# New order of the first two stages of a fused attention and feed-forward kernel: first chunk's squares ahead of all else on ScalarE, fewer dummy matmuls ahead of the first transposes

## Chip, cores, metric

One NeuronCore of a Trainium2 chip. The metric is the device time in microseconds (us) of one execution. Every run quoted here is of the fast state; a profile is of one such run. A ratio is the mean time of one kernel's fast runs over the mean of the other's in the same rounds, so it is not quite the ratio of the medians quoted beside it.

## What is computed

```python
# q, k, v: (8 batches, 12 heads, 448 rows, 64) float32
q_n, k_n = rmsnorm(q, g_q), rmsnorm(k, g_k)
attn = softmax(q_n @ k_n.T / 8) @ v                 # per batch and head
x = attn.transpose(0, 2, 1, 3).reshape(3584, 768)
h = x @ w_in                                        # 768 -> 2048
g = h + sin(alpha * h)**2 / (alpha + 1e-9)
out = g @ w_out                                     # 2048 -> 768
```

## The kernel before

It works batch by batch. Four heads of one batch are a *chunk*; batch b has chunks 3b, 3b+1, 3b+2 (counting from 0). The program order is not computed: it is written down as a *plan*, a string of tokens for batch 0 (STAGE_0), batch 1 (STAGE_1) and the rest (STAGE_N), a string of PSUM slots, and a table of tasks beside the first product. The first digit of most tokens is the chunk within the batch, 3 to 5 being the next batch's.

| token | engine | what |
|---|---|---|
| `L`, `G` | PE, then VectorE or ScalarE | spread alpha, spread g over the partitions |
| `l3` | SP | issue the loads of a chunk's q and k |
| `q30`, `q31` | ScalarE (chunks 0, 1), else GpSimd | squares of q, of k |
| `u30`, `u31` | VectorE | their row sums |
| `r3` | ScalarE | inverse root |
| `g3` | GpSimd | fold the gains g_q g_k into q, in place |
| `k30`, `k31` | VectorE (chunks 0 to 3), else GpSimd | scaled q, k in bf16 |
| `p3`, `t3` | PE with copies, or DMA | transpose |
| `S`, `S4` | PE, ScalarE | a score tile and its exponential; 4 dummy matmuls first |
| `b11` | PE | 11 dummy matmuls |
| `o v x y z` | PE | steps of (ones or values) x exponentials |
| `F` (a number: so many), `f` | PE | a filler: 8 matmuls of the batch before's second product |
| `W`, `O`, `V` | GpSimd | issue loads of w_in, w_out, v |
| `D2` | GpSimd | *gate*: copy one column of a chunk's k |

The gate does no arithmetic that anyone uses. GpSimd stops at it until that chunk's k has landed, so the weight loads that follow in GpSimd's order are issued later. In the changed kernel's profile only `D1` waits so: when `D2` and `D4` run (27.05 and 63.47 us), the k that they read has long landed (11.60 and 27.55). The parts that matter below (cuts marked ...):

```python
inp = ctx.enter_context(tc.tile_pool(name="inp", bufs=3))      # q and k of three chunks
...
    def load_qk(ci, k_queue=nc.sync):
        ...
        qk[ci] = inp.tile([P, 2, 2 * NJ, D], F32, tag="qk", name="qk")
...
        def square(w):
            if ci < 2:
                ...
                nc.scalar.activation(st.sq[w], qk[ci][:, w], ACT.Square)
            else:
                st.sq[w] = npool.tile([P, 2 * NJ, D], F32, tag="sq", name="sq")
                nc.gpsimd.tensor_mul(st.sq[w], qk[ci][:, w], qk[ci][:, w])
...
    def snake(b, ps, m):
        ...
        nc.scalar.activation(s1, hps, ACT.Sin, scale=alpha_sb[:, m, :])
        if m % 2 == 0:
            nc.gpsimd.tensor_mul(s2, s1, s1)
        else:
            nc.scalar.activation(s2, s1, ACT.Square)
        def finish():
            nc.vector.scalar_tensor_tensor(g_sb[...], s2, inv_alpha_sb[:, m, :], hps, ...)
            if m % 2:
                give_back(ps)          # PE may use the PSUM slot again
...
            if what == "D":
                nc.gpsimd.tensor_copy(gate, qk[ci][:, 1, 0, 0:1])
```

Three chunk buffers in turn: chunk 5's loads go where chunk 2 lies, chunk 7's where chunk 4 lies. A load waits until the last reader of the old chunk is done, and a gate is a reader.

The softmax here doesn't subtract the row's maximum and nothing guards it: scores larger than these inputs give would overflow.

Of the kernel before, what the change touches and what calls it, by code (L numbers as in the profile page):

```python
# [17 lines left out]
try:  # L18
# [12 lines left out]

STAGE_0 = (
    (
        "L G b11 q00 u00 q01 g0 b15 r00 u01 k00 r01 D1 k01 V00 q11 u11 p00 q10 V02 W11 p011 S4 u10 q20 r1 "
        "g1 S4 q21 S1 l3 u20 S1 k11 k10 S4 u21 S g2 r2 p1 k20 S2 V01 S2 S o3 q30 S W00 W12 k21 l4 o4 D2 "
        "q40 W01 p2 l5 S1 g4 S u30 q31 W02 g3 u40 v1 q41 S v6 u31 S S S3 S1 S3 x2 W10 S S x1 S1 u41 x2 y2 "
        "q51 y3 x2 z1 z1 y2 z1 z1 q50 r4 r3 z2 z1 O00 k31 "
    ),
    "2122130230213212301301321032130132012120312031230",
    {-1: 'u50 k30 u51 O01', 1: 'k401 O10', 2: 'k410 k411', 3: 'O11', 4: 'V10', 5: 'k400', 6: 'D4 l6 V11', 7: 'p3', 8: 'V12 g5 l7 p4'},  # L40
)
STAGE_1 = (
    (
        "q30 6 r2 1 S 4 S 1 S 2 S 2 u30 S k21 1 q41 1 S 1 f S 1 k20 1 S 1 S 1 f 1 S 1 f f f S q31 p2 1 "
        "u31 f l5 S 2 g3 S 2 S r3 2 u41 k30 V10 S 1 q40 1 V11 q50 S o7 v7 1 S k31 1 u40 S 2 S 3 S S 1 x6 "
        "r4 k41 z2 q51 x1 t3 y7 z5 "
    ),
    "13230103120101013131312310202302301230123",
    {-1: 'g4 V12', 1: 'k40', 3: 'u50 g5', 5: 'l6 u51', 8: 't4 l7'},
)  # L50
STAGE_N = (
    (
        "1 r2 q31 q30 f 2 S V10 f 3 V11 f f k20 2 S 3 S 2 k21 S u31 q40 1 t2 1 g3 1 S 1 f u30 S 2 f S f S "
        "r3 q41 f f 1 l5 1 f S 4 u40 S S 5 S S u41 o7 v7 S S 5 S 2 q51 f S 2 S q50 k31 k30 2 S g4 1 u50 S "
        "2 r4 t3 1 S z3 x7 k40 y7 z1 z2 z1 "
    ),
    "01232302102020301301320321310130210231023",
    {-1: 'l6 u51 V12', 1: 'k41', 2: 't4 l7', 3: 'g5'},
)
LAST = "0123012"  # L60

# [546 lines left out]
```

## Time and profile before

417.23 us median of 4 runs (416.84 to 417.42); the profiled span is 414.8 us.

| engine | busy share | what it does most |
|---|---|---|
| PE (TensorE) | 97% | products, scores, attention |
| ACT (ScalarE) | 76% | exponentials, sines |
| POOL (GpSimd) | 69% | squares, scalings, issues of loads |
| DVE (VectorE) | 55% | sums, copies out of PSUM |

The prediction shows the stretches, the chain and the run-in. Read so: over the whole span PE is the bound, but not in the first 39 us.

### The profile page before, as it was taken

Reading aid. Unit: us, or ns where it says so; the run is one execution under the profiler, and the core shown is the slowest. Engines: PE = TensorE matmul, PEld = TensorE weight load, DVE = VectorE, ACT = ScalarE, POOL = GpSimd, SP = SyncE. Lnnn points to the kernel's source line nnn. Section 1 sums busy time; section 2 is a strip of 40 time slices with the busy share of each in tenths; the row PEclk is TensorE's granted clock in tenths of the full one; section 3 lists DMA queues with packets and bytes.
Section 4 is the critical chain, followed back from the end, with each engine's and each line's share of the span. In section 5 each row is a group of like instructions: output and inputs, shape, how many; then the busy total and the mean of one; then the engine's idle time right before and its main releaser. Section 6 shows DMA issues by size and latency. Waiting matters only on the chain.

```text
span 414.8 us, 14996 instructions
## 1 busy us (share of the span) xinstructions
PE 403.4 (97%) x6657; PEld 238.9 (58%) x6657; DVE 227.2 (55%) x335; ACT 316.8 (76%) x465; POOL 285.0 (69%) x269
## 2 busy tenths in 40 slices
PE   4999999999999999999999999999999999999995
PEld 2344567655666557655666557655676556665563
DVE  2783774737754565655674565564565464435512
ACT  3698788968888689868889679878889688887600
POOL 3998998898869679498786879697794884003300
PEclk9999999999999999999999999999999999999999
DMA  8999999776273645567294744645375611320022
GB/s 257 176 220 241 168 226 217 167 155 174 29 206 93 150 134 103 158 90 193 70 182 112 175 136 88 172 111 149 92 135 162 89 45 44 82 60 2 1 77 76
DMA packets 64901, 54.07 MB, mean 130 GB/s; under 512 B 36276, under 2 KB 60612, under 8 KB 64836
## 3 DMA queue, kind: packets, MB, share of 16 engines
q1 hardware_dynamic: 51378, 39.60, 36.2%
q0 software_dynamic: 12512, 11.81, 19.3%
q10 hardware_dynamic: 946, 1.70, 1.1%
q8 instruction: 52, 0.85, 0.9%
q14 instruction: 13, 0.11, 0.1%
HBM read 45.62 MB, written 11.01 MB: 137 GB/s over the span
## 4 chain that ended last, share of the span: by engine, by line
PE 94%; ACT 3%; DMA 1%; issue 0%; DVE 0%; POOLq 0%
PE hps L401 35%; PE ops L480 30%; PE av L361 13%; PE sc L335 7%; PE ops L461 5%; ACT expT L338 3%; PE ps L243 2%; DMA small<-in_moe_alpha_dram 1%; PE sc L331 1%; PE tp L313 1%; ACT rec L367 0%; ACT rec L366 0%; PE aps L216 0%; DVE osb L466 0%; PE gps L209 0%
## 5 line engine op out<-in xcount | busy, mean ns | idle before, releaser
L338 ACT ACTIVATE expT<-sc 128x896 bf16<-128x896 f32 x168 | 144.6, 918 | 15.7 <-PE sc L335 15.1
L401 PE MATMUL hps<-xT,w_in 128*128 128x448 bf16 x768 | 146.7, 353 | 0.0
L480 PE MATMUL ops<-w_out_sb,g_sb 64*64 64x384 bf16 x3072 | 146.5, 323 | 0.0
L401 PEld LDWEIGHTS <-w_in 128*128 128x128 bf16 x768 | 74.4, 98 | 71.7 <-issue 3.0
L387 DVE SCALAR_TENSOR_TENSOR g_sb<-s,inv_alpha_sb,hps 128x448 bf16<-128x448 f32 x128 | 81.1, 677 | 62.8 <-POOL s L382 62.4
L480 PEld LDWEIGHTS <-g_sb 64*64 64x64 bf16 x3072 | 89.8, 107 | 39.4 <-issue 2.5
L382 POOL TENSOR_TENSOR s<-s 128x448 f32<-128x448 f32 x64 | 59.4, 932 | 66.9 <-ACT s L379 43.9
L379 ACT ACTIVATE s<-hps,alpha_sb 128x448 f32<-128x448 f32 x128 | 74.5, 626 | 38.4 <-PE hps L401 34.7
L265 POOL TENSOR_TENSOR sq<-qk 128x896 f32<-128x896 f32 x44 | 73.4, 1677 | 29.0 <-DMA qk<-in_k_dram 27.9
L290 POOL TENSOR_TENSOR qkn<-qk,inv 128x448 bf16<-128x448 f32 x80 | 72.8, 938 | 4.2 <-ACT inv L281 2.0
L335 PE MATMUL sc<-qkT 64*64 64x448 bf16 x672 | 57.1, 352 | 0.4 <-DVE qkT L320 0.2
L486 DVE COPY osb<-ops 128x384 f32<-128x384 f32 x48 | 26.7, 557 | 50.3 <-PE ops L480 50.3
L268 POOL TENSOR_TENSOR qk<-qk,gg 128x896 f32<-128x896 f32 x24 | 50.2, 2091 | 2.2 <-ACT g_sb L262 2.2
L271 DVE TENSOR_REDUCE ms<-sq 128x14 f32<-128x896 f32 x44 | 47.0, 1078 | 8.0 <-POOL sq L265 8.0
L373 DVE TENSOR_TENSOR xT<-av,rec 128x896 bf16<-128x896 f32 x24 | 25.4, 1088 | 33.7 <-ACT rec L367 33.7
L384 ACT ACTIVATE s<-s 128x448 f32<-128x448 f32 x64 | 36.9, 577 | 3.0
L361 PE MATMUL av<-expT,vb 64*32 64x448 bf16 (+1 forms) x1120 | 36.8, 350 | 0.1
L335 PEld LDWEIGHTS <-qkT 64*64 64x64 bf16 x672 | 20.2, 107 | 13.4 <-issue 4.5
L487 DVE TENSOR_TENSOR osb<-osb,ops 128x384 f32<-128x384 f32 x48 | 26.6, 554 | 1.7
L361 PEld LDWEIGHTS <-vb 64*32 64x32 bf16 (+1 forms) x1120 | 19.2, 96 | 13.2 <-issue 2.7
L361 PE MATMUL av<-expT,ones 64*32 64x448 bf16 (+1 forms) x672 | 25.3, 350 | 0.2 <-ACT expT L338 0.2
L461 PE MATMUL ops<-w_out_sb,g_sb 128*128 128x384 bf16 x128 | 21.0, 326 | 0.0
(48 smaller groups left out, 185.6 us busy)
## 6 DMA issues: line engine op xcount, KB each, us to landing
out_dram<-osb SPq DMA_DIRECT2D x39, 192.0 KB, 3.1
qk<-in_q_dram SPq DMA_DIRECT2D x16, 448.0 KB, 4.6
qk<-in_k_dram SPq DMA_DIRECT2D x14, 448.0 KB, 4.9
qk<-in_q_dram SPq DMA_DIRECT2D x16, 224.0 KB, 4.1
qk<-in_k_dram SPq DMA_DIRECT2D x16, 224.0 KB, 5.0
vb<-in_v_dram POOLq DMA_DIRECT2D x16, 224.0 KB, 4.4
w_out_sb<-in_moe_w_out_dram POOLq DMA_DIRECT2D x4, 768.0 KB, 12.8
out_dram<-osb SPq DMA_DIRECT2D x26, 96.0 KB, 3.6
```

The lines of the kernel that those rows point to most:

```text
L265: nc.gpsimd.tensor_mul(st.sq[w], qk[ci][:, w], qk[ci][:, w])
L268: eng.tensor_mul(qk[ci][:, 0], qk[ci][:, 0], gg.to_broadcast([P, 2 * NJ, D]))
L271: nc.vector.reduce_sum(st.ms[:, w, :], st.sq[w], axis=AX.X)
L290: eng.tensor_mul(n[:, :, hi, :], x[:, hi], inv[:, hi].unsqueeze(2).to_broadcast([P, NJ, D]))
L335: nc.tensor.matmul(sc[pp * 64:pp * 64 + 64, hi, :S], qkt[r, 1, j * REST:(j + 1) * REST], qkt[r, 0, :], start=True, stop=True)
L338: nc.scalar.activation(expT[c, j], sc[:, :, :S], ACT.Exp, scale=SCALE)
L361: nc.tensor.matmul(av[o, k, :S], w, expT[b * NC + c, j][r, hi, :], start=(j == 0), stop=(j == NJ - 1))
L379: nc.scalar.activation(s1, hps, ACT.Sin, scale=alpha_sb[:, m, :])
L382: nc.gpsimd.tensor_mul(s2, s1, s1)
L387: nc.vector.scalar_tensor_tensor(g_sb[:, m, (b % 2) * S:(b % 2 + 1) * S], s2, inv_alpha_sb[:, m, :], hps, op0=ALU.mult, op1=ALU.add)
L401: nc.tensor.matmul(ps[:, m % 2, :S], w_in_sb[m * 2 // MT][:, kt, m % (MT // 2) * P:(m % (MT // 2) + 1) * P], x[:, kt, :], start=(kt == ORD ...
L480: nc.tensor.matmul(st["ps"][os, r, :HALF], g_sb[rs, m, c0 + o * 64:c0 + o * 64 + 64], w_out_sb[rs, m, half * HALF:(half + 1) * HALF], star ...
```

## The change

The intent, as the diff reads: start batch 0 sooner. The first chunk's squares come first on ScalarE (`q01 q00` ahead of `G`, which holds the copy of g), the 15 dummies of `b15` go, two weight loads come first on GpSimd (`W02`, `W12`). Batch 1 does all its transposes by DMA. The plans of the later batches are new too, and so are the slots.

```diff
 STAGE_0 = (
     (
-        "L G b11 q00 u00 q01 g0 b15 r00 u01 k00 r01 D1 k01 V00 q11 u11 p00 q10 V02 W11 p011 S4 u10 q20 r1 "
-        "g1 S4 q21 S1 l3 u20 S1 k11 k10 S4 u21 S g2 r2 p1 k20 S2 V01 S2 S o3 q30 S W00 W12 k21 l4 o4 D2 "
-        "q40 W01 p2 l5 S1 g4 S u30 q31 W02 g3 u40 v1 q41 S v6 u31 S S S3 S1 S3 x2 W10 S S x1 S1 u41 x2 y2 "
-        "q51 y3 x2 z1 z1 y2 z1 z1 q50 r4 r3 z2 z1 O00 k31 "
+        "L q01 q00 G D1 u01 r01 u00 q11 W02 k01 b11 g0 q10 W12 r00 p011 q21 u11 k00 u10 g1 p00 q20 u21 r1 "
+        "k11 S4 S V00 g2 k10 V01 S2 u20 S1 l3 S3 q30 r2 p1 l4 S V02 S2 k20 k21 S1 S1 S3 S2 W00 S o7 W01 "
+        "p2 W11 b2 S D2 S S u30 v7 q41 W10 S S O01 u41 S1 q40 u40 l5 S1 q31 x3 S S1 z3 V10 O00 z2 x4 g3 "
+        "u31 y7 z2 r4 q51 r3 "
     ),
     ...
-    {-1: 'u50 k30 u51 O01', 1: 'k401 O10', 2: 'k410 k411', 3: 'O11', 4: 'V10', 5: 'k400', 6: 'D4 l6 V11', 7: 'p3', 8: 'V12 g5 l7 p4'},
+    {-1: 'k31 k30 g4', 0: 'q50 l6', 1: 'k401', 2: 'u50', 3: 'O10 k410', 5: 'k411 u51 k400', 7: 'g5 D4', 8: 'O11 p3 p4 V12 V11 l7'},
 )
 STAGE_1 = (
     (
-        "... S 1 f 1 S 1 f f f S q31 p2 1 u31 f l5 S 2 g3 ... "
+        "... f 1 S k21 f 1 S f t2 1 S 3 f S 1 u31 ... g3 f 1 S 1 V10 r3 l5 S g4 ... x2 u50 x4 x1 y1 l6 q51 ... "
     ),
     ...                                                  # slots, STAGE_N: new orders of the same work
```

## Prediction

> **What bounds the kernel now.** I read the page's table of busy shares first (PE 97%, ScalarE 76%, GpSimd 69%), then stretches cut at the borders of the stages, then the timeline of the first 40 us, then the chain that ended last. A stage is one batch: attention (21 score tiles, interleaved with the second product of the batch before), then the first product. Busy time of each engine by stretch; the columns are the stretch, its length, PE, PEld, DVE, ACT, POOL, the clock, DMA share, GB/s:
>
> ```profile
> 17.43:37.37 19.94, 18.97 (x305) 8.22 (x304) 13.61 (x20) 19.82 (x27) 18.91 (x17) 1.00 1.03 239
> 59.16:87.22 28.06, 28.02 (x723) 18.94 (x721) 16.31 (x26) 24.80 (x34) 24.62 (x23) 1.00 0.89 183
> 105.55:134.87 29.32, 29.24 (x758) 19.44 (x758) 16.25 (x25) 26.34 (x36) 24.34 (x20) 1.00 0.48 116
> 153.14:182.18 29.04, 29.04 (x757) 19.49 (x758) 15.96 (x25) 26.07 (x36) 22.90 (x19) 1.00 0.48 108
> 200.44:229.49 29.05, 29.05 (x758) 19.50 (x758) 15.97 (x25) 26.07 (x36) 22.48 (x19) 1.00 0.51 107
> ```
>
> Two regimes. In the attention of the first batch (17.43 to 37.37, first exponential to the end of the last) ScalarE is busy 19.82 of 19.94 us: it is the bound, and PE's 18.97 holds dummy matmuls that only fill its waits. From the second batch on PE is never idle. To see whether "busy" there means "issuing at full rate", I count starts. From the chain:
>
> ```profile
> 39.50 18.27 PE hps L401 x96
> 202.06 2.60 PE ops L480 x64
> 223.71 0.33 PE ops L480 x8
> 225.39 4.10 PE av L361 x168
> ```
>
> A filler (8 second-product matmuls) costs 2.60/8 = 0.325 us, a first product 18.27, three both-chunk attend passes 4.10. The PE timeline gives 0.19 us per score tile (201.70 to 201.89) and 1.32 per seven-step ones or values pass, of which a batch has two. A steady batch has 56 fillers: 56 x 0.325 + 21 x 0.19 + 2 x 1.32 + 4.10 = 28.9 us against 29.04 measured. There is nothing left to win there except a loss avoided. The second batch has 48 fillers and one transpose group on PE (28 transposes, 0.82 us): 15.6 + 3.99 + 2.64 + 4.10 + 0.82 = 27.15 against 28.06: 0.9 us is lost in short stalls. The third lost 0.3 (29.32). So the time is: start of the first product of batch 0 (39.5), then a PE-bound remainder. The run-in, by the timeline (start, length, engine, line):
>
> ```profile
> 7.21 1.79 ACT L262 ACTIVATE g_sb<-qk 128x896 f32<-128x896 f32 x2
> 8.25 2.08 POOL L268 TENSOR_TENSOR qk<-qk,gg 128x896 f32<-128x896 f32 x1 [2.19 <-ACT g_sb L262]
> 10.36 2.21 DVE L290 TENSOR_TENSOR qkn<-qk,inv 128x448 bf16<-128x448 f32 x4
> 7.00 8.33 PE L243 MATMUL ps<-blank 128*128 128x512 bf16 x26
> 15.26 0.69 PE L313 MATMUL tp<-ident,qkn 64*128 64x64 bf16 x28
> 15.78 0.69 DVE L320 COPY qkT<-tp 128x448 bf16<-128x448 bf16 x2 [2.21 <-PE tp L313]
> 16.85 0.53 PE L335 MATMUL sc<-qkT 64*64 64x448 bf16 x4
> 17.43 0.92 ACT L338 ACTIVATE expT<-sc 128x896 bf16<-128x896 f32 x1 [0.47 <-PE sc L335]
> ```
>
> Both halves of the first chunk were scaled at 12.57 (10.36 + 2.21), but the transposes started at 15.26, because 26 dummies stood ahead of them. That is 2.7 us lost on the path, and DVE's wait of 2.21 on the transposes is its mark. The squares began at 7.21, although the landing events in the trace put the first chunk's q at 5.22 and k at 5.51: they stood behind the copy of g (7.11), which waits for a matmul.
>
> **What the Trainium skill says.** "TensorE: Matmul & The Clock Gate", Part 1: the clock is half until some 3.4 us of sustained activity; what counts is time, not a number of matmuls. The trace agrees roughly: dummies issue every 0.42 us up to about 11.7 and every 0.21 us (14 in 2.90) after, some 4.7 us from 7.0. So 11 dummies are just enough. The same page, back-to-back issue gap: N/2.4 + 2.5 ns, 189 ns at 448; the trace has 18.27/96 = 190. "ScalarE: Activation LUTs", What ACT_TABLE_LOAD costs: 186 ns + 0.833 N, less 93 when back to back, 839 ns at N = 896; the trace has 0.82 (11 in 8.99). "DMA: Bandwidth & Descriptors", SWDGE vs HWDGE vs iDMA: both kinds feed different queues of the same engines, served in turn; so a weight load issued earlier can slow the q and k loads. The trace shows a DMA share near 1.0 in this stretch, so that is possible.
>
> **The change part by part.**
>
> *Run-in.* ScalarE squares k then q from 5.55: 5.55 + 1.79 = 7.34, 1.66 earlier than before (9.00). The g matmul now shares a PSUM slot with alpha's, so waits for DVE's copy (6.77), ends about 7.45, and the copy of g at 7.66. DVE reduces k and q after alpha's reciprocal (7.06): 2.08, to 9.14. k's inverse root on ScalarE 8.15 to 8.68; scale k 9.14 + 1.10 = 10.25. The second chunk's squares come before q's inverse root: its k lands at 8.83, so 8.87 + 1.77 = 10.64, root 11.2.
>
> GpSimd, though, has its gate (L536, a copy that waits for the second chunk's k at 8.83) and one weight load (0.73) put before the fold of g into q: 8.85 + 0.18 + 0.75 + 2.08 gives 11.9, where it was done at 10.33 before. DVE: second chunk's k reduced 10.25 to 11.3, q scaled 11.95 to 13.05, another reduction to 14.1, then the two copies of the q transposes, 0.69: 14.8. PE: 11 dummies cold, 7.45 + 11 x 0.427 = 12.15; k's transposes to 12.6; q's 13.1 to 13.5; four dummies to 14.6; first scores 14.85. Before: 16.85. First exponential 0.58 later: 15.4 against 17.43. So half of what the squares and dummies give (up to 4 us) is spent on the fold behind the gate, and the shift is 2.0 us.
>
> *ScalarE's stream.* Before, between first exponential and end of last: 21 exponentials, two inverse roots of 0.49, one reciprocal pair of 1.83: 19.94 us. Now one of the roots stands before the first exponential, where ScalarE waits anyway: 19.45. Last exponential ends 15.4 + 19.45 = 34.9, 2.5 earlier. Feeders: the third chunk's q square on GpSimd ends about 18.05, its reduction 19.15, and its root is due after five exponentials, at 19.5: just in time. Second chunk transposed about 20.3, due 21.7. Third: fold 20.9, scaled 23.1, ample.
>
> *Tail.* Before, 2.1 us from the last exponential to the first product. Now 18 attend steps (3.5 us) stand after the last scores on PE, with the last ones step waiting for the last exponential. Last scores about 33.6 (two exponentials before the end, since slots are short): 33.9 + 3.5 gives 37.4. First product 37.5 against 39.5: **2.0 us**.
>
> *First product of batch 0.* Same PE work, 18.27. GpSimd now enters it with a fold, a square that waits for a load, and another fold still queued; I put its end near 43.3 where the first snake square is due near 42.4. PSUM slots three to four tiles deep hide some 2 us of that: I allow **0.3 us** of loss.
>
> *Second batch.* The transpose group goes from PE to a DMA: **0.8 us** off. Of the 0.9 lost in short stalls I give the new order **0.4**. Steady batches: same 56 fillers, 21 scores, same totals, no gain.
>
> Sum: -2.0 + 0.3 - 0.8 - 0.4 = -2.9; I shade it by 0.1 for the unseen: 417.17 - 2.8 = **414.4 us**, 0.7% faster. Of the 18 dummies removed (53 become 35) only the 15 ahead of the first transposes count; those among the scores filled PE's waits on ScalarE.
>
> **Rivals.**
> 1. *The gate takes the whole gain.* If the weight load issued at 9.1 slows the second or third chunk's loads, or GpSimd falls behind, the root due at 19.5 comes late and ScalarE idles 1 to 2 us. For it: GpSimd is busy 18.91 of 19.94 there and the DMA queues are full. Against: the third chunk had landed at 9.95 (q) and 11.77 (k), mostly before the new load moves data. Time: 415.5 to 416.5.
> 2. *PE stays cold.* If 11 dummies miss the clock window, the transposes and first scores run at half rate. Against: ScalarE is the bound there, and half-rate scores (0.4 us) still outrun it. Costs at most 0.5 us.
> 3. *The new steady order makes a wait.* Six batches, so 0.3 us each is 1.8 us, and it would bring 416. I compared the PE work ahead of each score tile in both orders; the new one reaches some tiles sooner (the fourteenth by 2.7 us: 15.5 against 18.1 us into the batch), but none before ScalarE, at 0.82 us a tile from about 3.2 us, has come so far; four slots lie between. The third tile is the tight one (4.28 us after the product's end; ScalarE free near 4.1). Likely loss 0 to 0.1 each.
> 4. *Better than I think.* No stalls in batch 1 (0.9), none in batch 2 (0.3), the tail waiting on ScalarE alone (37.2): 413.2.
>
> **Range and chances.** Best sensible sum 412.8, rivals 1 and 3 together 416.5: range 412.7 to 416.4. Faster by 2% would need 8.3 us, more than the run-in holds beyond its PE work; slower by 2% needs 1.4 us of new stalls in each of six batches, against the count above. Faster 0.02, within 2% 0.96, slower 0.02.
>
> **What would show each step.** Right if: squares start near 5.6; the fold of g starts near 9.8; first exponential near 15.4; ScalarE busy over 97% from there to a last exponential near 34.9; first product near 37.5; no transposes on PE in the second batch, and its attention near 26.9; steady batches at 47.3. Wrong if an idle time of ScalarE over 0.5 us stands before an inverse root or exponential in the first batch, if the first products of batch 0 have PE idle on GpSimd's squares, or if steady batches are longer than 47.5.

## Result

The changed kernel takes **420.89 us** median of 4 runs (419.01 to 420.95): ratio 1.0078, 95% interval 1.0049 to 1.0107. It is 0.8% slower. Predicted were 414.4 us and a range from 412.7 to 416.4, so the time lies outside the range, on the other side of the kernel before.

The stretches of the changed kernel (same columns as in the prediction: stretch, length, PE, PEld, DVE, ACT, POOL, clock, DMA share, GB/s):

```profile
15.20:34.66 19.46, 17.27 (x294) 8.04 (x299) 12.33 (x18) 19.36 (x25) 18.96 (x19) 1.00 1.04 219
36.83:59.68 22.85, 19.86 (x104) 9.66 (x97) 13.79 (x20) 14.30 (x27) 17.68 (x16) 0.93 1.11 206
61.22:88.67 27.45, 27.36 (x691) 20.00 (x692) 15.11 (x23) 23.43 (x31) 23.94 (x22) 1.00 0.84 174
88.95:109.54 20.59, 18.59 (x105) 9.30 (x98) 12.20 (x18) 13.84 (x25) 15.11 (x16) 1.00 0.80 168
156.92:185.89 28.97, 28.97 (x757) 19.54 (x757) 15.38 (x24) 26.49 (x36) 25.00 (x20) 1.00 0.56 115
```

The first line is batch 0's run of exponentials: it starts 2.2 us sooner and ScalarE is its bound as before. The second and fourth are the first products of batches 0 and 1, 18.3 us each before and now 22.85 and 20.59: in both PE is idle, and the second has a granted clock of 0.93. The last is a steady attention stretch, as tight as before.

The run-in (start, length, engine, line):

```profile
5.58 1.79 ACT L262 ACTIVATE g_sb<-qk 128x896 f32<-128x896 f32 x2 [1.96 <-DMA qk<-in_k_dram]
7.40 4.33 PE L243 MATMUL ps<-blank 128*128 128x512 bf16 x11
9.87 2.09 POOL L268 TENSOR_TENSOR qk<-qk,gg 128x896 f32<-128x896 f32 x1
13.20 0.48 PE L313 MATMUL tp<-ident,qkn 64*128 64x64 bf16 x14 [1.06 <-DVE qkn L290]
14.06 0.68 DVE L320 COPY qkT<-tp 128x448 bf16<-128x448 bf16 x2
15.20 4.16 ACT L338 ACTIVATE expT<-sc 128x896 bf16<-128x896 f32 x5 [0.48 <-PE sc L335]
```

This is the predicted chain within a few tenths: squares at 5.58 (5.55), fold at 9.87 (9.8), q's transposes at 13.2 (13.1), first exponential at 15.2 (15.4). PE now waits for the scaling; before, the scaled tiles waited for PE's dummies.

The gain is lost after that. Start and end of the first products; "no_both_gates" is an experiment below:

| | before | changed | difference | no_both_gates |
|---|---|---|---|---|
| first product of batch 0 starts | 39.43 | 36.83 | -2.60 | 37.25 |
| its length | 18.27 | 22.85 | +4.58 | 18.26 |
| to the next first product | 29.52 | 29.27 | -0.25 | 29.44 |
| length of batch 1's | 18.26 | 20.59 | +2.33 | 18.45 |
| to batch 2's first product | 29.32 | 29.04 | -0.28 | 29.04 |
| batch 2's first product starts | 134.80 | 138.58 | +3.78 | 132.44 |

From there to the end it is 280.0 us before and 280.5 after; in that stretch PE stops once, 0.60 us at 232.3. So all of the loss but 0.5 us is two stops of PE, one in each of the first two first products.

**First stop.** The timeline of the changed kernel, SP, GpSimd and PE:

```profile
27.05 0.19 POOL L536 COPY gate<-qk 128x1 f32<-128x1 f32 x1
27.27 2.10 SPq L161 DMA_DIRECT2D qk<-in_q_dram  x2
29.42 1.54 SPq L161 DMA_DIRECT2D qk<-in_k_dram  x2
36.41 2.11 POOL L268 TENSOR_TENSOR qk<-qk,gg 128x896 f32<-128x896 f32 x1
43.12 1.67 POOL L265 TENSOR_TENSOR sq<-qk 128x896 f32<-128x896 f32 x1 [4.61 <-DMA qk<-in_k_dram]
44.76 2.07 POOL L268 TENSOR_TENSOR qk<-qk,gg 128x896 f32<-128x896 f32 x1
46.79 0.93 POOL L382 TENSOR_TENSOR s<-s 128x448 f32<-128x448 f32 x1
49.08 10.67 PE L401 MATMUL hps<-xT,w_in 128*128 128x448 bf16 x48 [2.99 <-DVE g_sb L387]
```

Chunk 5's loads are issued right after gate D2 has run (27.05 + 0.19). The last of its k lands at 42.96 by the trace's landing events; before, it was 39.11. GpSimd stands idle 4.61 us for it, squares it, does the fold that was queued behind, and starts the first snake square at 46.79, where the sine was ready at about 41.8. Until VectorE has finished that tile no PSUM slot is free, and PE starts no matmul from 45.73 to 49.08, which costs 3.15 us (3.34 less the usual 0.19). The 48 matmuls after it took 10.67 us, where the 48 before it took 9.25: 1.4 us more, with eight starts 0.373 us apart instead of 0.19 and a half clock in the clock record for 3.4 us. Stop and half clock together are the 4.6 us.

**Second stop.** In batch 1, GpSimd, VectorE and PE:

```profile
88.72 1.68 POOL L265 TENSOR_TENSOR sq<-qk 128x896 f32<-128x896 f32 x1 [2.77 <-DMA qk<-in_q_dram]
90.43 1.08 DVE L271 TENSOR_REDUCE ms<-sq 128x14 f32<-128x896 f32 x1 [4.69 <-POOL sq L265]
91.43 2.08 DVE L373 TENSOR_TENSOR xT<-av,rec 128x896 bf16<-128x896 f32 x2
92.57 0.73 PE L401 MATMUL hps<-xT,w_in 128*128 128x448 bf16 x3 [1.93 <-DVE xT L373]
```

Again a late load (chunk 8), GpSimd's square behind it, a reduction on VectorE behind that, the multiplication that makes PE's operand behind the reduction. The loads had been issued at 82.6; the same chunk's at 72.4 before.

**What held the loads.** SP's own waits from 15 to 66 us (waiting instruction, what released it, us in total, times, longest), before:

```profile
SPq L158 <- POOL gate L536: 11.8, 1, 11.8
SPq L161 <- DVE qkn L290: 3.6, 1, 3.6
```

Changed:

```profile
SPq L158 <- POOL gate L536: 20.8, 1, 20.8
SPq L161 <- POOL gate L536: 4.1, 1, 4.1
```

L161 is chunk 5's load. Before, it waited last for the scaling of chunk 2, the work that empties the buffer; gate D2, at 25.3, was already over. Now the scaling is done at 23.1 and the gate comes at 27.05, because it stands behind more work in GpSimd's order: the gate holds the load 4.1 us. L158 with its long wait is chunk 7's load, held by D4 until 63.7 (58.0 before). Of its 20.8 us only the end is the gate's own, since the load also needs the scaling of chunk 4. On GpSimd:

```profile
57.14 1.83 POOL L290 TENSOR_TENSOR qkn<-qk,inv 128x448 bf16<-128x448 f32 x2
63.47 0.18 POOL L536 COPY gate<-qk 128x1 f32<-128x1 f32 x1
```

The scaling is done at 58.97, the gate at 63.65: D4 holds the load 4.7 us.

### The profile page after: what moved, and what is told of

The parts are those of the page before. It is cut to its first block, busy times and chain, and to the rows that moved or that the text cites. A ratio compares the mean times of both kernels' runs of the same rounds, so it can differ in the third digit from the quotient of the medians.

```text
span 419.1 us, 14910 instructions
## 1 busy us (share of the span) xinstructions
PE 400.2 (95%) x6607; PEld 239.4 (57%) x6611; DVE 225.3 (54%) x333; ACT 316.1 (75%) x465; POOL 285.6 (68%) x269
## 4 chain that ended last, share of the span: by engine, by line
PE 80%; POOL 8%; DMA 6%; DVE 2%; SPq 1%; issue 1%; ACT 0%; ACTq 0%; POOLq 0%
PE hps L401 29%; PE ops L480 29%; PE av L361 10%; PE sc L335 6%; PE ops L461 5%; DMA qk<-in_k_dram 5%; POOL qk L268 2%; POOL sq L265 2%; DMA qk<-in_q_dram 1%; DVE g_sb L387 1%; POOL s L382 1%; POOL qkn L290 1%; SPq L161 1%; SPq L451 1%; DVE ms L271 1%
## 5 line engine op out<-in xcount | busy, mean ns | idle before, releaser
L401 PE MATMUL hps<-xT,w_in 128*128 128x448 bf16 x768 | 148.6, 355 | 5.0 <-DVE g_sb L387 3.0
L480 PE MATMUL ops<-w_out_sb,g_sb 64*64 64x384 bf16 x3072 | 149.6, 323 | 0.0
L480 PEld LDWEIGHTS <-g_sb 64*64 64x64 bf16 x3072 | 91.4, 107 | 38.4 <-issue 2.4
L335 PE MATMUL sc<-qkT 64*64 64x448 bf16 x672 | 60.0, 352 | 1.8 <-DVE xT L373 1.1
L361 PEld LDWEIGHTS <-vb 64*32 64x32 bf16 (+1 forms) x1120 | 20.3, 96 | 12.5 <-issue 2.1
```

The source lines that it names most:

```text
L335: nc.tensor.matmul(sc[pp * 64:pp * 64 + 64, hi, :S], qkt[r, 1, j * REST:(j + 1) * REST], qkt[r, 0, :], start=True, stop=True)
L361: nc.tensor.matmul(av[o, k, :S], w, expT[b * NC + c, j][r, hi, :], start=(j == 0), stop=(j == NJ - 1))
L401: nc.tensor.matmul(ps[:, m % 2, :S], w_in_sb[m * 2 // MT][:, kt, m % (MT // 2) * P:(m % (MT // 2) + 1) * P], x[:, kt, :], start=(kt == ORD ...
L480: nc.tensor.matmul(st["ps"][os, r, :HALF], g_sb[rs, m, c0 + o * 64:c0 + o * 64 + 64], w_out_sb[rs, m, half * HALF:(half + 1) * HALF], star ...
```

## Experiments

Times are medians of fast runs; "before" is the kernel before in the same jobs (416.7 to 417.4 us). The columns FP 0 and FP 1 are the length of batch 0's and batch 1's first product beyond 18.27 us.

| run | us | ratio to before, 95% | FP 0 | FP 1 |
|---|---|---|---|---|
| changed kernel | 420.89 | 1.0078 (1.0049 to 1.0107) | +4.6 | +2.3 |
| stage0_only | 422.07 | 1.0121 (1.0068 to 1.0173) | +2.8 | 0.0 |
| later_only | 420.81 | 1.0082 (1.0060 to 1.0105) | +0.3 | 0.0 |
| square_late | 419.48 | 1.0053 (1.0035 to 1.0071) | +3.3 | +2.2 |
| no_gate | 417.35 | 1.0010 (0.9991 to 1.0030) | 0.0 | +2.3 |
| nogate_load_early | 421.76 | 1.0108 (1.0056 to 1.0160) | 0.0 | 0.0 |
| nogate_reduce_late | 416.55 | 0.9983 (0.9966 to 1.0000) | 0.0 | +2.4 |
| nogate_pe_transpose | 428.41 | 1.0266 (1.0249 to 1.0283) | +0.4 | 0.0 |
| before_no_b15 | 417.32 | 0.9994 (0.9978 to 1.0011) | +4.0 | 0.0 |
| transpose_later | 416.06 | 0.9968 (0.9949 to 0.9988) | +0.2 | 0.0 |
| transpose_later_no_d4 | 414.08 | 0.9931 (0.9908 to 0.9954) | 0.0 | 0.0 |
| nogates_old_later | 414.31 | 0.9936 (0.9911 to 0.9961) | 0.0 | 0.0 |
| fold_first | 414.93 | 0.9942 (0.9921 to 0.9962) | +0.8 | 0.0 |
| no_both_gates | 413.96 | 0.9940 (0.9924 to 0.9956) | 0.0 | +0.2 |
| no_both_gates_reduce_late | 414.17 | 0.9943 (0.9924 to 0.9962) | 0.0 | 0.0 |

All gave correct results. A gate is a copy into a tile that nobody reads, so taking one away frees no data that something else needs; each kernel passed the check before the chip.

The two right columns are read from one profiled run each, and some kernels scatter: no_gate from 415.8 to 419.5 us (profiled 416.9), stage0_only in two groups near 420.4 and 424 (profiled 420.4), nogate_load_early from 419.7 to 423.9 (profiled 423.5), before_no_b15 from 416.3 to 419.2 (profiled 419.1). What makes the scatter was not looked into.

### Which batch loses: stage0_only and later_only

```diff
# stage0_only: the changed kernel with        # later_only: the kernel before with
-STAGE_1, STAGE_N of the changed kernel       -STAGE_1, STAGE_N of the kernel before
+STAGE_1, STAGE_N of the kernel before        +STAGE_1, STAGE_N of the changed kernel
```

> New plan for batch 0, old plans for the later batches. In the changed kernel batch 0 starts its first product 2.6 us earlier than before (36.8 against 39.4) but ends it 2.0 us later (59.7 against 57.7), since PE stands 3.3 us and then runs cold. If the loss of batch 1 (2.3 us in its first product) belongs to batch 1's own new order, this kernel keeps only the 2.0 us of batch 0: about 419.2 us, and batch 1's first product takes 18.3 us. Rival: if batch 1 loses because batch 0 hands it everything late, the loss comes with the old order too: 420.5 to 421.5 us.

> Old plan for batch 0, new plans for the later batches. If batch 1's loss is its own: its first product still has a gap near 2 us before the xT multiplication on VectorE has run, 418.5 to 419.2 us. Rival, inherited loss: no gap, the transposes off PE save 0.8 us and the third batch 0.3: 416.0 to 416.6 us.

Neither came out as expected, and neither separates the batches. At the seam PE stops 1.84 us in one (59.1) and 3.21 us in the other (58.5): the second plan begins with a PSUM slot that the first plan's last snake still holds. The slot strings are fitted to one another across the seam, which I had not seen when I cut there. In stage0_only PE stops 2.85 us more, at a transpose group that waits for GpSimd's scaling. The two show only that a plan's start depends on the end of the plan before it.

### The first stop: square_late and no_gate

```diff
# square_late, batch 0: a square and a fold behind the first snake squares
-... y7 z2 r4 q51 r3    {-1: 'k31 k30 g4', 0: 'q50 l6', 1: 'k401', 2: 'u50', 3: 'O10 k410', ...}
+... y7 z2 r4 r3        {-1: 'k31 k30', 0: 'q50 l6', 1: 'g4', 2: 'q51 u50', 3: 'O10 k401 k410', ...}
```

> The changed kernel with two GpSimd operations of batch 0 moved behind the first snake squares: the square of the sixth chunk's k (which waits for a load that landed at 43.0) and the fold of g into the fifth chunk's q. Theory: PE's stop at 46 us is the in-order GpSimd queue standing behind that load; it vanishes with its cold clock, 4 to 4.6 us: 416.3 us, lower (414) if batch 1's loss was inherited. Rival: the stop comes from the new order of PSUM slots in the first product (one slot held by an inverse root until two scalings are done, reuse three tiles deep); the slots are the same here, so PE still stops over 2 us: 419 to 421 us.

The wait for the load went: GpSimd starts the first snake square at 42.27. But PE stops all the same, 3.09 us at 53.1, and only the half clock is saved. GpSimd had been idle 3.5 us ahead of 42.27, and the 3.8 us of moved work now stands between the snake squares. GpSimd has 17 to 18 us of work beside batch 0's first product of 18.3 us, so what it loses to a late load ahead of it cannot be put off into it. A miss: 419.5 us and a stop of over 2 us are what the rival said (419 to 421), not the theory (416.3). But the rival's mechanism, the slots, is ruled out by the next run, which has the same slots.

```diff
# no_gate, batch 0
-p2 W11 b2 S D2 S S u30 v7 ...
+p2 W11 b2 S S S u30 v7 ...
```

> The changed kernel without the second GpSimd gate (a copy of one column that reads the third chunk's buffer at 27.05 and so holds back the load of the sixth chunk into that buffer). Gate theory: the sixth chunk's loads are issued from about 23.2 us (end of the third chunk's scaling) instead of 27.3, its k lands before 39.5, and PE's stop shrinks to under 1 us: 416 to 417 us. Rival, crowding theory: the weight loads issued from 24 to 31 us share the DMA engines and k still lands after 41.5; the stop stays over 1.5 us: 419 to 421 us.

One token gone, and the first stop with it; the total, 417.35 us, is a little over the expected 416 to 417. Chunk 5's loads are issued at 23.1, its k lands at 34.92. The stretches of batch 0's and batch 1's first product in no_gate:

```profile
36.74:54.92 18.18, 18.18 (x104) 9.31 (x96) 13.83 (x20) 14.24 (x27) 17.24 (x16) 1.00 1.23 226
84.92:105.38 20.46, 18.49 (x104) 9.29 (x96) 12.10 (x17) 13.85 (x25) 15.08 (x16) 1.00 0.79 163
```

PE is never idle in the first, and as idle as in the changed kernel in the second. So the crowding by weight loads, which stand in the same places as in the changed kernel, does not by itself make the stop, and batch 1's loss is not handed down from batch 0's.

### The second stop, tried in batch 1: nogate_load_early, nogate_reduce_late, nogate_pe_transpose

```diff
# nogate_load_early (batch 1)                 # nogate_reduce_late (batch 1)
-... S f t2 1 S 3 f ... r3 l5 S g4 ...        -... V12 z1 x2 u50 x4 x1 y1 ... k40 z2
+... S f t2 l5 1 S 3 f ... r3 S g4 ...        +... V12 z1 x2 x4 x1 y1 ... k40 z2 u50
```

> The gateless kernel (417.4 us, batch 0 clean, batch 1's first product with a gap of 2.25 us), with one more edit: in batch 1 the issue of the last chunk's loads stands right behind the DMA transposes on the SP queue instead of behind three pairs of stores. Theory: those loads, issued at 78.1 and landed at 84.5 and later, hold GpSimd's squares, through them a reduction on VectorE, and through that the xT multiplication that PE waits for. Issued near 73 they land before 80 and the gap goes: batch 1's first product 18.2 to 18.6 us, total 414.8 to 415.5 us. Rival: the gap is VectorE's own backlog (output copies and reductions), the loads do not matter: gap over 1.5 us, 417 us.

The stop in the first product went, and a worse one came: 5.7 us at 80.0. VectorE's wait there, and PE's behind it:

```profile
DVE osb L486 <- DMA out_dram<-osb: 7.8, 1, 7.8
PE sc L335 <- DVE osb L487: 5.4, 1, 5.4
```

SP issues in order: now the stores stood behind transposes and loads, output tiles did not come free, VectorE could not empty PSUM, and PE had no slot. So the run does not test the theory of the late load: the loads, issued from 74.19, still landed as late as 83.89, and the first product began only at 94.23, 9.3 us later than in no_gate.

> The gateless kernel with one reduction of batch 1 moved behind the two xT multiplications in VectorE's order; the loads stay late. Theory: the gap of 2.25 us before PE's 9th matmul of the first product is that reduction, waiting for GpSimd; it vanishes. But GpSimd still works off the late chunk until 93.5, so the first snake squares are late and PE may stop some 0 to 1.5 us further on: 415.3 to 416.8 us. Rival (the multiplication itself is late because its reciprocal is): the gap stays, 417.4 us.

The gap at the 9th matmul went, as the theory says, and came back as one of 2.10 us at 93.7, at the snake squares of a late GpSimd. The loss moved from one waiter on GpSimd to the next; I had expected 0 to 1.5 us.

```diff
# nogate_pe_transpose (batch 1), with a PSUM slot for it
-... k21 f 1 S f t2 1 S ...
+... k21 f 1 S f p2 1 S ...
```

> The gateless kernel with batch 1's first chunk of transposes on PE as in the kernel before, instead of by DMA. Theory: the DMA transposes wait on the SP queue (from 62.5 to 69.9) for GpSimd's scaling and hold stores and loads behind them; without them the stores leave as they are ready, the loads are issued before 75, both small stops (0.6 us each) and the gap of 2.25 us go, at a price of 0.8 us on PE: 414.5 to 415.8 us. If the queue is not what held them, the price alone shows: 418.2 us.

This tests nothing of the queue: the place fits a DMA that may wait, not PE. PE's timeline:

```profile
66.93 0.38 PE L313 MATMUL tp<-ident,qkn 64*128 64x64 bf16 x7 [2.49 <-POOL qkn L290]
71.94 1.08 PE L313 MATMUL tp<-ident,qkn 64*128 64x64 bf16 x21 [4.64 <-POOL qkn L290]
```

PE, in order, stood 7.1 us for GpSimd's scaling. It shows what the DMA transposes hide.

### The third gate: transpose_later, transpose_later_no_d4, nogates_old_later

```diff
# transpose_later = nogate_reduce_late and, in batch 1
-... S f t2 1 S 3 f S 1 u31 1 S 3 S 1 o2 S o5 u41 ... V10 r3 l5 S g4 ...
+... S f 1 S 3 f S 1 u31 1 S 3 S 1 o2 S o5 t2 l5 u41 ... V10 r3 S g4 ...
# transpose_later_no_d4: also, beside batch 0's first product
-7: 'g5 D4',
+7: 'g5',
```

> Gateless kernel with the late reduction (416.6 us; in batch 1, PE stops 2.1 us in the first product for GpSimd's late squares), with one more edit: in batch 1 the DMA transposes stand some 5 us later in program order and the last chunk's loads right behind them. Theory: on the SP queue the transposes waited from 62.8 to 70.0 for GpSimd's scaling and held stores that were ready; then loads stood behind the held stores. Now stores up to about 70 leave in time, the loads are issued by 74 and land by 81, GpSimd no longer waits for them (2.8 us before), the stop of 2.1 us shrinks to under 0.5: 414.2 to 415.0 us. Rival: GpSimd itself has too much to do between 62 and 93 us (it is busy all but 4 us), then the stop shrinks by no more than half: 415.6 to 416.6 us.

> As transpose_later, without the third gate of GpSimd too (it reads the fifth chunk's buffer at 59.1 and so holds back the eighth chunk's loads, whose k GpSimd waits for 0.95 us at 66.5). Theory: those loads are issued near 54.3, where the scaling of the fifth chunk ends, GpSimd's wait goes, and what follows on GpSimd and SP comes 1 us earlier: batch 1's first product without a stop over 0.5 us, 0.3 to 1 us less than transpose_later. Rival: more loads at that time delay the second product's weights, the fillers of batch 1 stop: no gain or a loss.

With the later transposes alone the first product is clean, but PE stops 2.1 us at 75.7 for the transposes: they wait for GpSimd's scaling, 2.3 us late with the load of chunk 7's k. 416.06 lies in the rival's range, though the stop in the first product went as the theory says. Without gate D4 that load is issued at 54.2 instead of 59.3, and no PE gap over 0.5 us is left in batches 0 and 1: 414.08, 2.0 us less, more than the 0.3 to 1 expected.

```diff
# nogates_old_later: batch 0 of the changed kernel without D2 and D4, then the old plans
-STAGE_1, STAGE_N, LAST of the changed kernel
+those of the kernel before, PSUM slots renamed 1<->2, 3<->0
```

> The new plan of batch 0 without the second and third gates, followed by the old plans of all later batches, with the PSUM slots of those renamed so that they follow on from batch 0 as the new plans do (the first mixed kernels did not do this, and PE stopped 1.8 and 3.2 us at the seam for a slot). Theory: nothing at the seam; batch 0 ends at 54.9, 2.7 us earlier than before. If the old order of batch 1 has only its own small stops, 414.4 us; if it lives from GpSimd having 2.7 us more time (its transposes on PE wait for GpSimd's scaling), a stop of 1 to 2.5 us at those transposes: 415.5 to 417 us.

414.31: the seam costs 0.65 us, and nothing else stops. The old and the new plans of the later batches are worth the same once batch 0 hands over in time. So the new order of batch 1 is not what made the kernel slower.

### The two gates alone: no_both_gates, no_both_gates_reduce_late

```diff
-p2 W11 b2 S D2 S S u30 v7 ...        -..., 7: 'g5 D4', ...
+p2 W11 b2 S S S u30 v7 ...           +..., 7: 'g5', ...
```

> The changed kernel without the second and third gates and nothing else. If the third gate is the cause in batch 1 too: the eighth chunk's loads issued near 54, batch 1's first product without its gap, 413.9 to 414.7 us. If the order of transposes, stores and loads on the SP queue is a cause by itself: the gap of 2.25 us shrinks only by the 1 us that GpSimd gains, 415.4 to 416.6 us.

> As no_both_gates, with the reduction of batch 1 behind the two xT multiplications. If loads are in time, no difference (413.9 to 414.7). If they are late, the gap moves from the 9th matmul of the first product to a later one, as it did with one gate left, and shrinks by no more than 0.5 us: 415 to 416.4 us.

Without the two gates and with nothing else touched the changed kernel takes 413.96 us, 0.6% less than the kernel before and 6.9 us less than the changed one. Stretches that hold its first products of batches 0 and 1, and SP's waits:

```profile
36.70:55.42 18.72, 18.72 (x128) 9.43 (x104) 13.83 (x20) 14.79 (x27) 18.08 (x16) 1.00 1.23 226
84.95:103.31 18.36, 18.34 (x102) 9.30 (x96) 11.38 (x17) 13.64 (x25) 12.98 (x14) 1.00 0.81 177
```

```profile
SPq L158 <- POOL qkn L290: 11.3, 1, 11.3
SPq L161 <- DVE qkn L290: 4.0, 1, 4.0
```

Both loads now wait for the scaling that empties their buffer and nothing else. With that, the place of batch 1's reduction makes no difference (414.17), as expected. The two gates are the whole of the regression. No run took D4 alone out of the changed kernel.

How D4 makes the second stop is shown only in part. Chunk 8's loads are issued at 77.93, hardly earlier than in no_gate (78.13), since on SP they still stand behind the DMA transposes and six stores. But the last of its q landed at 82.41 instead of 84.50, and GpSimd squared it 2.1 us sooner. Chunk 7's k, for which GpSimd had waited 1.17 us in no_gate, had landed at 61.04 instead of 66.37. Why chunk 8's loads then took some 2 us less is not resolved.

### The run-in: before_no_b15 and fold_first

```diff
# before_no_b15: the kernel before, batch 0    # fold_first = transpose_later_no_d4, batch 0
-L G b11 q00 u00 q01 g0 b15 r00 ...            -L q01 q00 G D1 u01 r01 u00 q11 W02 k01 b11 g0 q10 ...
+L G b11 q00 u00 q01 g0 r00 ...                +L q01 q00 G g0 D1 u01 r01 u00 q11 W02 k01 b11 q10 ...
```

> The kernel before with nothing changed but the second row of 15 dummy matmuls ahead of the first transposes left out. Theory of the prediction: the transposes had been ready at 12.6 and start there instead of at 15.3; the first exponential near 14.9 instead of 17.4, the first product near 37.0 instead of 39.4, and the rest as before unless the sixth chunk's loads, whose landing (39.1) does not move, now come too late for GpSimd: 414.8 us if they do not, 416 to 417.2 if they do.

The first exponential came at 14.42 and the first product at 36.43, 3.0 us sooner: the dummies alone were worth more than the whole new order's 2.6. The time did not move: PE stops 2.4 us at 38.6 and runs 1.8 us long after it (in the profiled run, which took 419.1 us; the median is 417.32).

```profile
41.03 17.75 PE L401 MATMUL hps<-xT,w_in 128*128 128x448 bf16 x84 [2.04 <-DMA w_in<-in_moe_w_in_dram]
```

Not chunk 5's load, as I had thought, but a part of w_in: `W02`, issued at 30.8 and landed at 40.98. The new order has W02 first, which fits. By this trace the old dummies cost nothing because this load was the next bound; no run moved W02 alone to show it.

> As transpose_later_no_d4, and in the run-in the fold of g into the first chunk's q ahead of GpSimd's first gate and weight load. By the prediction's chain the fold then ends near 9.9 instead of 11.9, the q scaling waits for its inverse root (11.2) instead, and the first exponential moves from 15.2 to 14.4; the weight load is issued about 1 us later. Theory: 0.8 us off the start of batch 0's first product, and off the total if nothing later is bound by a load: 0 to 0.8 us less than transpose_later_no_d4. Rival: the loads keep their times and take it back (as in the kernel before without its 15 dummies): no change.

The fold starts at 7.96 and the first exponential at 14.45, 0.8 us sooner, as computed. The first product starts at 36.96, no sooner: PE waits 1.19 us just ahead of it for a part of w_in (issued at 24.55, landed at 36.91), and stops 0.86 us at 52.8. The total is 414.93 (413.65 to 415.25) against 414.08 (413.71 to 414.72): no gain, the rival's case.

## Why the prediction was wrong

By its steps:

- **Run-in and ScalarE's stream: right.** First exponential 15.20 (15.4), end of the last 34.66 (34.9), ScalarE busy 19.36 of 19.46 us, first product 36.83 (37.5, so 0.7 us better). That the squares' gain is partly spent on the fold behind the gate is shown by fold_first, but for 0.8 us, not for the half of 4 us that the prediction put down to it.
- **"First product of batch 0 ... I allow 0.3 us of loss": the step that failed.** It measured 4.6. The text said that GpSimd would enter with "a square that waits for a load", and put GpSimd's end near 43.3 without working out when that load is issued. It was held by gate D2 until 27.27, landed at 42.96, and GpSimd came free of it at 46.8. The diff shows D2 in its new place, and the old profile has a wait of SP on a gate (L158, 11.8 us). I had taken the gate for an order of GpSimd's issues and not for a reader of a buffer. no_gate takes the term to 0.0.
- **"Second batch: -0.8, -0.4": wrong in sign.** It lost 2.1 (-0.25 and +2.33). The transposes left PE, but gate D4 held chunk 7's loads to 63.7, GpSimd waited for them, and chunk 8's loads came late. no_both_gates takes this to +0.1, not to -1.2: some 1 us of small stops remains there that I did not resolve. Part of it may be the order on the SP queue: that stretch is 28.95 us in transpose_later_no_d4 against 29.44 in no_both_gates. This is not shown, since the totals do not differ (414.08 and 413.96).
- **Steady batches: right in the main.** From one first product to the next, three of five took 47.31 us, as before; the others took 47.91 (with the stop at 232.3) and 47.49.
- **Rivals.** The first named the gate, but D1 and the run-in. The second (a cold PE) did not happen in the run-in; half clock came after the stop. The third did not happen, apart from the stop of 0.60 us.
- **The sum** of 414.4 us is what the change gives without the two gates (413.96), but by parts that do not match one by one: batch 1 gave 1.3 less, the first product's 0.3 of loss did not come, the third batch gave 0.3 (left out of the sum), the run's end another 0.2. The agreement is no proof of the sum.

## What to carry to other kernels

When work that feeds an engine moves forward, list every load that it will wait for and ask of each what releases its *issue*, from the queue's own waits, not only from the consuming engine's. Any instruction that reads a buffer, even one that exists only to order another engine's queue, holds the next load into it. In a run-in, taking away one wait pays only as far as the next landing (here a part of w_in at 41.0 in before_no_b15, chunk 5's k at 43.0 in the changed kernel), so look at the landing times before counting the gain.

## What the Trainium skill lacked or had wrong

- "TensorE: Matmul & The Clock Gate", Part 1 and its closing table: half clock after an idle window of about 3.4 us, so no idle gaps over some 3 us. Here the length of a stop did not decide it. Within 1.5 us after a stop of 2.39 us (before_no_b15) came nine starts 0.373 us apart, but none after stops of 2.85 us (stage0_only) and 3.09 us (square_late). What separates them is how a stop falls. In all 16 traces the clock records, but for the last of each, are whole multiples of 3.41 us long. Cut the stretches at full clock into windows of that length: in 21 of them (five within the run, one at the end of each) PE was idle for 2.04 us or more by the profile's modelled ends, and half clock follows each; it follows none of the 1866 others (idle 1.92 us at most). So a window need not be idle throughout. This comes from counting in the traces; no run was made to test it.
- "DMA: Bandwidth & Descriptors", Anatomy of one DMA: a fit of 2.0 us plus bytes over 436e3, measured on the SWDGE path. For 224 KB it gives 2.5 us (an estimate from the page). Chunk 5's last k load, issued by SP behind three loads of the same size and with the queues full, took 12.8 us from issue to landing in the changed kernel and 9.9 in no_gate; the first of the four took 9.4 and 5.5. For ordinary loads that share the engines I found no figure on the page.
- No page that I read says that a dummy read used to order one engine's queue also holds the next load into that buffer; here by 4.1 us (D2) and 4.7 us (D4).
